# Splitting the 128x128 matmuls of a graph propagation into four of 128x32, so that one stage of TensorE uses a single array shape

## The chip, the core and the metric

The kernel runs on one core of one Trainium2 chip. The metric is the device time of one execution in microseconds (us), as a median over several executions. Three executions of the kernel before took 3994.35, 3999.09 and 4004.58 us; their median is 3999.09 us.

## The reference

The input is a graph with N = 10000 nodes and E = 160000 edges, and a feature vector of D = 128 numbers for each node. The features are propagated seven times along the edges; each result is kept, and a small attention block then works on the eight vectors of each node.

```python
h = x
toks = [x]
for _ in range(7):
    msg = h[src] * deg_inv_sqrt[src, None] * deg_inv_sqrt[dst, None]
    h = _segment_sum(msg, dst, N)
    toks.append(h)
tok = jnp.stack(toks, axis=1)                      # (N, 8, D)
t = _layernorm(tok, axis=-1)
# q, key, v = t @ wq, t @ wk, t @ wv;  attn = softmax(q key^T / sqrt(D))
o = tok + (attn @ v) @ wo
alpha = softmax(layernorm(o) @ w_r)                # over the 8 tokens
out = sum over k of alpha[:, k] * o[:, k]
```

## The kernel before, in words

The program has four parts: a sort of the edges (up to about 420 us), hop 1 with the building of the matrices (to about 1200 us), hops 2 to 7 (to about 3297 us) and the attention (the rest). The change touches hops 2 to 7 alone.

A hop is written as matrix products with zeros and ones. The table `tab` of the node vectors lies in SBUF: 79 blocks of 128 nodes, each vector as a sum of two float16 halves, so 256 columns. The destinations are also taken in 79 tiles of 128 nodes, one pass of `block` (L492) for each. For one tile, 18 groups (`NG`) of up to 128 edges are handled in 9 pairs:

- **Gather** (L541): for each group four matmuls, each with a 128x32 piece of the matrix `w` as the stationary operand and one source block `tab[:, s, :]` (128x256) as the moving operand. They go to the four 32-row quarters of a PSUM tile `p`, so to the four 32-column strips of the array. There are 72 of them in a tile. The pool of `p` has six buffers (L636), and a tile takes nine, one for each pair.
- **Eviction** (L544): `p` is copied to SBUF as float16, `eb`, by ScalarE for the pairs 0, 2, 4, 5 and 7 and by VectorE for 1, 3, 6 and 8 (the rule is in the call at L701).
- **Scatter** (L517 in `scat`): for each group one matmul with a 128x128 piece of `w` and `eb` (128x256), summed up in the PSUM tile `acc`. There are 18 in a tile.
- **Fetched and overflow rows** (`fetched`, L503): two more 128x128 matmuls into `acc`, with rows `og` that GpSimd has fetched from the table in HBM by an indirect DMA (L488), one with a piece of `w` and one with the matrix `Sov`. In the first two tiles of a hop (`late`) the overflow matmul stands in `close` (L530) instead, since its rows are written only at the end of the hop before.
- **Closing** (L532 and `fin`, L675): VectorE adds the two halves to `s`, ScalarE scales it into the new table (L677), VectorE makes the second half (L678) and a maximum (L680), and ScalarE issues the DMA of the new rows to HBM (L158). For the blocks from 72 on it issues a second one, to `tabh` (L162); these seven tiles come first in a hop (`order`, L685). GpSimd scales `s` for the output (L573).

The order on TensorE follows from `block`: all 72 gathers of a tile, then the fetched and overflow matmuls, then what is left over of the tile before (its last four scatter matmuls, `lag` is 2 pairs), then 14 scatter matmuls of the tile itself. Each engine works through its own list in the order of the program, and waits on semaphores. The matrix `w` of a tile (592 KB) is loaded by a DMA on SyncE's queue (L700) into one of five buffers. `fetch` for the tile two ahead is held back by a small copy (L487) that waits for the eviction of pair 4.

Of the kernel before, what the change touches and what calls it, by code (L numbers as in the profile page):

```python
# [20 lines left out]
NG = 18  # L21
NI = 1
# [15 lines left out]
class Hops:  # L38
# [453 lines left out]
    def block(self, t, w, tab, og, pend, lag, runs, first, evac, fin, lead=False, late=False, mid=None, ahead=None):  # L492

        nc, V, A, T, G = self.nc, self.nc.vector, self.nc.scalar, self.nc.tensor, self.nc.gpsimd
        m = 257 if first else 256
        acc = []


        def fetched(i, start=False, stop=False):
            W = w[:, (NG + i) * 128:(NG + i + 1) * 128] if i < NI else self.Sov[:, t, :]
            T.matmul(acc[0][:, :256], W, og[i], start=start, stop=stop)  # L503
            if first:
                T.matmul(acc[0][:, 256:257], W, self.ones16, start=False, stop=False)

        def begin():
            acc.append(self.pacc.tile([128, 512], F32, name="acc", tag="acc"))
            for i in range(NI if late else NI + 1):
                fetched(i, start=i == 0)  # L510

        def scat(e, jj):
            if not acc:
                acc.append(self.pacc.tile([128, 512], F32, name="acc", tag="acc"))
            for j in range(e.shape[1]):
                J = 2 * jj + j
                T.matmul(acc[0][:, :m], w[:, J * 128:(J + 1) * 128], e[:, j, :m], start=first and J == 0,  # L517
                         stop=J == NG - 1 and not (first or late))
                if first and J == 0 and not lead:
                    for i in range(NI):  # L520
                        fetched(i)

        def close():
            if first:
                if lead:
                    for i in range(NI):
                        fetched(i)
                T.matmul(acc[0][:, 256:257], self.Sov[:, t, :], self.ones16, start=False, stop=False)
            if first or late:
                T.matmul(acc[0][:, :256], self.Sov[:, t, :], og[NI], start=False, stop=True)  # L530
            s = self.fp.tile([128, 128], F32, name="s")
            V.tensor_reduce(s, acc[0][:, 0:256].rearrange("p (h d) -> p d h", h=2), axis=X, op=ALU.add)  # L532
            fin(t, s, acc[0])

        def gather(jj):
            n = min(2, NG - 2 * jj)
            p = self.pg.tile([128, 2, 2, 128], F32, name="p")
            for j in range(n):
                for q in range(4):
                    s = 4 * (2 * jj + j) + q  # L540
                    T.matmul(p[32 * q:32 * q + 32, j], w[:, NJ * 128 + s * CAP:NJ * 128 + (s + 1) * CAP], tab[:, s, :], start=True, stop=True)  # L541
            e = self.ebuf[self.eb_i % len(self.ebuf)]
            self.eb_i += 1
            (A.copy if evac(jj) else V.tensor_copy)(e[:, :n, 0:256], p[:, :n].rearrange("p j h d -> p j (h d)"))  # L544
            pend.append(lambda: scat(e[:, :n], jj))

        jj = 0
        for i, n in enumerate(runs):
            for _ in range(n):
                gather(jj)  # L550
                if jj == 4 and not first and not mid:
                    ahead(self.ebuf[(self.eb_i - 1) % len(self.ebuf)][:, 0, 0:1])
                jj += 1
            if mid:
                mid(0)
            if not first:
                begin()
                if mid:
                    ahead()
            while len(pend) > lag:  # L560
                pend.pop(0)()
            if mid:
                mid(1)
            if i == len(runs) - 1:
                pend.append(close)
            yield
# [642 lines left out]
```

## Time and profile before

| | before |
|---|---|
| median of three executions | 3999.09 us |
| span of the profiled execution, first to last instruction | 3993.2 us |
| TensorE busy (matmuls) | 3698.2 us, 69691 matmuls |
| TensorE weight loads | 3031.4 us, 69691 |
| VectorE busy | 3307.4 us |
| ScalarE busy | 2652.0 us |
| GpSimd busy | 1775.7 us |

The device time of the profiled execution itself is not shown, only its span, which lies 1.2 us under the shortest of the three times. In the profile PE is TensorE's matmuls, PEld its weight loads, DVE is VectorE, ACT ScalarE, POOL GpSimd, SP SyncE; "ACTq" and the like are DMA issues by that engine. The profile models the end of a matmul, and matmuls overlap: one of 256 columns has 0.27 us in the trace though the next may start 0.11 us after it. So the pace of TensorE is to be read from starts, and its busy share says little.

### The profile page before, as it was taken

What the parts mean: (1) busy time and instruction counts of PE and PEld (TensorE: products, weight loads), DVE (VectorE), ACT (ScalarE), POOL (GpSimd) and SP (SyncE); (2) the same over time, 40 slices, a digit from 0 to 9 for tenths busy, and PEclk for the clock granted to TensorE, in tenths of its full rate; (3) what the DMA queues carried; (4) which work ended last, traced back from release to release, by engine and by line L of the source; (5) the groups of instructions that cost most, each with busy time, mean ns of one, the idle gap of its engine ahead of it and who ended that gap; (6) DMA issues with size and microseconds to landing.
All of it is one profiled execution on the core that took longest, in us unless ns stands there. A gap on an engine that the chain in (4) does not pass through costs nothing. (4 is left out here: it accounts for less than half of the span.)

```text
span 3993.2 us, 164299 instructions
## 1 busy us (share of the span) xinstructions
PE 3698.2 (93%) x69691; PEld 3031.4 (76%) x69691; DVE 3307.4 (83%) x6948; ACT 2652.0 (66%) x6799; POOL 1775.7 (44%) x2355
## 2 busy tenths in 40 slices
PE   4776799999979999999999999999999997999997
PEld 3765666667648888888888888888888886888875
DVE  8998999999967777777777777777766665999998
ACT  6774366666666666666666666666655557888884
POOL 0000333333326665666666666666656661222222
PEclk8988999999989999999999999999999998999998
DMA  3100444444456666666666666666656653222220
GB/s 107 30 1 1 129 152 153 146 153 149 145 179 198 201 200 196 202 202 203 192 203 203 195 201 201 202 199 203 203 182 187 188 168 91 76 78 78 75 74 13
DMA packets 320622, 594.87 MB, mean 149 GB/s; under 512 B 55623, under 2 KB 213541, under 8 KB 314629
## 3 DMA queue, kind: packets, MB, share of 16 engines
q1 hardware_dynamic: 219749, 477.37, 38.5%
q0 software_dynamic: 35392, 72.55, 6.0%
q10 hardware_dynamic: 64736, 34.38, 3.0%
q8 instruction: 546, 8.95, 0.9%
q14 instruction: 199, 1.63, 0.1%
HBM read 455.43 MB, written 128.67 MB: 146 GB/s over the span
## 5 line engine op out<-in xcount | busy, mean ns | idle before, releaser
L544 ACT CAST eb<-p 128x512 f16<-128x512 f32 x3081 | 1591.0, 602 | 694.6 <-PE p L541 670.7
L544 DVE CAST eb<-p 128x512 f16<-128x512 f32 x1896 | 1179.3, 683 | 346.7 <-PE p L541 331.1
L541 PE MATMUL p<-tab,w 128*32 128x256 f16 x39816 | 1284.9, 274 | 39.8 <-ACT eb L544 22.1
L517 PE MATMUL acc<-eb,w 128*128 128x256 f16 (+1 forms) x9954 | 1239.8, 273 | 12.7 <-DVE indeg L595 10.3
L541 PEld LDWEIGHTS <-w 128*32 128x32 fp8e4 x39816 | 1001.3, 96 | 240.1 <-issue 181.6
L517 PEld LDWEIGHTS <-w 128*128 128x128 fp8e4 x9954 | 953.1, 98 | 174.5 <-issue 61.6
L488 POOL DMA_INDIRECT og<-tabh,oidx x553 | 638.4, 1154 | 732.4 <-DVE vi L440 400.6
L488 POOL DMA_INDIRECT og<-tabd,oidx x541 | 563.3, 1041 | 433.8 <-PE acc L530 268.3
L573 POOL TENSOR_SCALAR r<-s,ctok 128x128 f32<-128x128 f32 x474 | 296.1, 625 | 33.6 <-DVE s L532 18.5
L678 DVE SCALAR_TENSOR_TENSOR tab<-s,c,tab 128x128 f16<-128x128 f32 x395 | 139.2, 352 | 183.1 <-ACT tab L677 182.1
L677 ACT ACTIVATE tab<-s,c 128x128 f16<-128x128 f32 x395 | 158.5, 401 | 182.7 <-DVE s L532 182.4
L487 POOL COPY og<-eb 128x1 f16<-128x1 f16 x457 | 85.1, 186 | 426.7 <-ACT eb L544 426.6
L315 ACT ACTIVATE o<-oh,d2s 128x79 f16<-128x79 f16 x800 | 204.7, 373 | 80.9 <-PE ta L329 80.9
L532 DVE TENSOR_REDUCE s<-acc 128x128 f32<-128x256 f32 x553 | 228.5, 413 | 27.4 <-PE acc L530 20.4
L918 ACT ACTIVATE junk<-x 128x128 f32<-128x128 f32 x625 | 245.0, 394 | 0.0
L476 DVE TENSOR_TENSOR w<-dsl,iof 128x2432 fp8e4<-128x2432 f16 x79 | 211.7, 2679 | 0.0
L976 POOL TENSOR_TENSOR p<-e,in 128x512 f32<-128x512 f32 (+1 forms) x40 | 40.8, 1021 | 342.8 <-DVE e L974 342.8
L904 PEld LDWEIGHTS po<-v,pT 128*128 128x128 f32 x1250 | 159.0, 193 | 44.7 <-issue 27.6
L329 PE MATMUL ta<-o,ro 128*128 128x158 f16 x1250 | 119.7, 267 | 77.9 <-DVE ro L325 77.8
L893 PE MATMUL pv<-Wv,xT 128*128 128x131 f32 x1250 | 175.7, 284 | 4.5 <-ACT xT L873 3.8
L329 PEld LDWEIGHTS <-ro 128*128 128x128 f16 x1250 | 114.5, 113 | 82.2 <-DVE ro L325 82.0
L904 PE MATMUL po<-v,pT 128*128 128x128 f32 x1250 | 166.8, 277 | 7.7 <-DVE o L910 7.7
(277 smaller groups left out, 4642.3 us busy)
## 6 DMA issues: line engine op xcount, KB each, us to landing
w<-gsd SPq DMA_DIRECT2D x474, 592.0 KB
gsd<-w SPq DMA_DIRECT2D x79, 592.0 KB
rb<-srow SPq DMA_DIRECT2D x79, 576.0 KB
tok<-r SPq DMA_DIRECT2D x546, 64.0 KB
x<-tok SPq DMA_DIRECT2D x266, 128.0 KB
tabd<-tab ACTq DMA_DIRECT2D x395, 64.0 KB
og<-tabh,oidx POOLq DMA_INDIRECT x553
og<-tabd,oidx POOLq DMA_INDIRECT x541
```

The source lines that it names most:

```text
L315: A.activation(o[:, j - a, NK:, i], oh[:, j, :, i], AF.Copy, scale=d2s[:, c0:c0 + 1])
L329: T.matmul(ta, ro[:, j - a, :, i], o[:, j - a, :, i], start=j + i == 0, stop=j + i == NP)
L476: V.tensor_tensor(w[:, :NJ * 128].rearrange("p (j d) -> p j d", d=128), dsl[:, g, :, None].to_broadcast([128, NJ, 128]), self.iof1[:, None ...
L488: self.nc.gpsimd.indirect_dma_start(out=o, out_offset=None, in_=src[0] if i == NI else src[1], in_offset=bass.IndirectOffsetOnAxis(ap=self ...
L517: T.matmul(acc[0][:, :m], w[:, J * 128:(J + 1) * 128], e[:, j, :m], start=first and J == 0, stop=J == NG - 1 and not (first or late))
L532: V.tensor_reduce(s, acc[0][:, 0:256].rearrange("p (h d) -> p d h", h=2), axis=X, op=ALU.add)
L541: T.matmul(p[32 * q:32 * q + 32, j], w[:, NJ * 128 + s * CAP:NJ * 128 + (s + 1) * CAP], tab[:, s, :], start=True, stop=True)
L544: (A.copy if evac(jj) else V.tensor_copy)(e[:, :n, 0:256], p[:, :n].rearrange("p j h d -> p j (h d)"))
L573: self.nc.gpsimd.tensor_scalar(r, s, ct[:, t:t + 1], None, op0=ALU.mult)
L893: T.matmul(p[:, g - a, :], S[i]["xT"][:, g, :], Wv, start=True, stop=True)
L904: T.matmul(p[:, g - a, :], PT[i % 2][:, g, :], S[i]["v"][:, g, :128], start=True, stop=True)
L918: A.activation(j, S[i]["x"][:, g, :], AF.Square, bias=S[i]["x"][:, g, 0:1], scale=-1.0, accum_out=S[i]["sq"][:, g:g + 1])
```

## The change

A helper `onto` takes the place of the plain call in the three places that write `acc`. In hop 1 (`first`) it makes the same single matmul as before. In hops 2 to 7 it makes four: column strip c of the stationary matrix, 32 columns wide, goes to the strip c of the array and to the rows c to c + 31 of `acc`. All four have the same moving operand, and the flags `start` and `stop` of the one that they replace. In these hops the 20 matmuls of 128x128 in a tile become 80 of 128x32, as the gathers already are; the numbers that are added stay the same.

```diff
+        def onto(W, rhs, start, stop):
+
+            if first:
+                T.matmul(acc[0][:, :rhs.shape[-1]], W, rhs, start=start, stop=stop)
+                return
+            for c in range(0, 128, 32):
+                T.matmul(acc[0][c:c + 32, :rhs.shape[-1]], W[:, c:c + 32], rhs, start=start, stop=stop, tile_position=(0, c))
+
         def fetched(i, start=False, stop=False):
             W = w[:, (NG + i) * 128:(NG + i + 1) * 128] if i < NI else self.Sov[:, t, :]
-            T.matmul(acc[0][:, :256], W, og[i], start=start, stop=stop)
+            onto(W, og[i], start, stop)
...
                 J = 2 * jj + j
-                T.matmul(acc[0][:, :m], w[:, J * 128:(J + 1) * 128], e[:, j, :m], start=first and J == 0,
-                         stop=J == NG - 1 and not (first or late))
+                onto(w[:, J * 128:(J + 1) * 128], e[:, j, :m], first and J == 0, J == NG - 1 and not (first or late))
...
             if first or late:
-                T.matmul(acc[0][:, :256], self.Sov[:, t, :], og[NI], start=False, stop=True)
+                onto(self.Sov[:, t, :], og[NI], False, True)
```

## The prediction

> **What bounds the kernel now.** I read the page first, for the share of each engine over time.
>
> ```profile
> span 3993.2 us, 164299 instructions
> PE 3698.2 (93%) x69691; PEld 3031.4 (76%) x69691; DVE 3307.4 (83%) x6948; ACT 2652.0 (66%) x6799; POOL 1775.7 (44%) x2355
> PE   4776799999979999999999999999999997999997
> L517 PE MATMUL acc<-eb,w 128*128 128x256 f16 (+1 forms) x9954 | 1239.8, 273 | 12.7 <-DVE indeg L595 10.3
> q8 instruction: 546, 8.95, 0.9%
> w<-gsd SPq DMA_DIRECT2D x474, 592.0 KB
> ```
>
> Each slice is 100 us, and a queue has packets, MB and its share. PE shows 9 through hops 2 to 7, which are 474 tiles (one load of `w` each). A busy PE isn't yet a bound, so I next asked for the engines in stretches inside each of the six hops.
>
> ```profile
> core 0: us, PE busy (x) PEld busy (x) DVE busy (x) ACT busy (x) POOL busy (x), PEclk, DMA share, GB/s
> 1240.00:1540.00 300.00, 300.00 (x6307) 254.44 (x6300) 230.96 (x482) 202.39 (x413) 190.80 (x275) 1.00 0.65 202
> 1650.00:1890.00 240.00, 240.00 (x5060) 203.74 (x5059) 184.57 (x385) 161.94 (x330) 152.96 (x220) 1.00 0.65 202
> 1965.00:2240.00 275.00, 275.00 (x5796) 233.37 (x5795) 211.50 (x441) 185.51 (x378) 175.07 (x252) 1.00 0.65 202
> 2295.00:2400.00 105.00, 105.00 (x2224) 89.19 (x2220) 80.65 (x168) 70.74 (x145) 66.85 (x98) 1.00 0.65 203
> 2410.00:2590.00 180.00, 180.00 (x3800) 152.61 (x3789) 138.65 (x289) 121.59 (x249) 113.97 (x164) 1.00 0.65 203
> 2645.00:2940.00 295.00, 295.00 (x6210) 250.32 (x6203) 227.34 (x474) 199.11 (x407) 187.29 (x269) 1.00 0.65 202
> 3005.00:3290.00 285.00, 284.88 (x5996) 241.46 (x5989) 183.71 (x327) 165.93 (x328) 179.58 (x259) 1.00 0.59 182
> ```
>
> PE is covered throughout, at clock 1.00; DVE has 77%, ACT 67%, POOL 64%, the DMA engines 65%. The stretches hold 35393 matmuls; at 92 for a tile that is 385 tiles in 1680 us, 4.37 us each. Third, the timeline of one such tile shows what the 4.37 us consist of.
>
> ```profile
> 2408.41 2.15 PE L541 MATMUL p<-tab,w 128*32 128x256 f16 x72
> 2408.92 2.54 ACT L544 CAST eb<-p 128x512 f16<-128x512 f32 x5 [1.00 <-PE p L541]
> 2409.08 2.48 DVE L544 CAST eb<-p 128x512 f16<-128x512 f32 x4 [0.58 <-PE p L541]
> 2410.49 0.28 PE L503 MATMUL acc<-og,w 128*128 128x256 f16 x1
> 2410.61 0.27 PE L503 MATMUL acc<-og,Sov 128*128 128x256 f16 x1
> 2410.72 2.13 PE L517 MATMUL acc<-eb,w 128*128 128x256 f16 x18
> ...
> 2411.49 0.41 DVE L532 TENSOR_REDUCE s<-acc 128x128 f32<-128x256 f32 x1
> 2411.93 0.40 ACT L677 ACTIVATE tab<-s,c 128x128 f16<-128x128 f32 x1 [0.47 <-DVE s L532]
> 2412.37 0.35 DVE L678 SCALAR_TENSOR_TENSOR tab<-s,c,tab 128x128 f16<-128x128 f32 x1 [0.47 <-ACT tab L677]
> 2412.63 0.28 DVE L680 TENSOR_REDUCE mx<-tab 128x1 f32<-128x128 f16 x1
> 2412.75 0.33 ACTq L158 DMA_DIRECT2D tabd<-tab  x1
> ...
> 2412.78 0.84 PE L541 MATMUL p<-tab,w 128*32 128x256 f16 x24
> ```
>
> A row's length runs from the first start to the last modelled end. The 18 scatter matmuls take 2.13 us, the last of them 0.273, so 17 steps take 1.857: 0.1092 us each. The 72 gathers go in 18 sets of four that start nearly together (four strips of the array at once): (2.15 - 0.273)/17 = 0.110 for a set. Gathers and scatters thus cost the same, one slot of 0.109, and a tile has 18 + 20 = 38 slots: 38 x 0.1092 = 4.15 us. The period is 4.37. The missing 0.22 us sits at the two seams. The last scatter starts at 2410.72 + 1.86 = 2412.58 and the next gather at 2412.78: 0.20, not 0.11. The last gather set starts at 2408.41 + 2.15 - 0.27 = 2410.29, the first matmul of 128x128 at 2410.49: 0.20 again. The rest, about 0.02, is a slower first slot behind each seam (2410.49 to 2410.61 is 0.12). The list of waits says whether every tile pays this.
>
> ```profile
> PEld L503 <- issue: 98.9, 468, 0.2
> PEld L541 <- issue: 93.6, 440, 0.9
> PEld L541 <- DMA tok<-r: 10.5, 50, 0.2
> PE acc L530 <- DMA ogl<-tabd,oidx: 9.1, 5, 3.9
> ```
>
> Before L503 the weight loader is idle 468 times, 0.21 us each; before L541 490 times, 0.21 each. It is the same at both seams, though different things could be waited for there, and nearly always put down to no releaser. I take it that TensorE empties itself when the shape of the tiles in the array changes.
>
> **The change, part by part.** *Seams.* With one shape in hops 2 to 7 both go. A tile shrinks from 4.37 to 38 x 0.1092 = 4.15 us, by 0.22. For the 385 tiles of the stretches that is 84.7 us.
>
> *Tiles outside the stretches*, 474 - 385 = 89, are mostly the starts of the hops. One of those:
>
> ```profile
> 2262.25 2.29 PE L541 MATMUL p<-tab,w 128*32 128x256 f16 x72
> 2262.47 0.45 ACTq L162 DMA_DIRECT2D tabh<-tab  x1
> 2263.02 2.54 ACT L544 CAST eb<-p 128x512 f16<-128x512 f32 x5 [1.33 <-PE p L541]
> ...
> 2266.76 0.62 PE L541 MATMUL p<-tab,w 128*32 128x256 f16 x16
> ```
>
> Here ACT issues a second DMA, its first eviction starts 0.77 us after the first gather (0.51 in the tile above), and the gathers take 2.29 instead of 2.15: they wait for one of the six `p`. The period is 4.51. ACT's loop sets it together with PE: its restart counts from the gather start before, so what PE saves in one period comes back as a later `p` in the next, and on average half is kept, 0.11 of 0.22. Tiles that wait for a fetch (L530, five times) keep nothing. Between 0 and 0.22 for each of the 89, I take 0.14, most of them being between these ends: 12 us. Together 84.7 + 12 = 97 us.
>
> *The split matmuls themselves* are new: 128x32, float8 weights, four with the same moving operand, adding to `acc`. Nearest rows:
>
> ```profile
> 3409.53 0.83 PE L893 MATMUL pv<-Wv,xT 128*128 128x131 f32 x6
> 3410.30 0.64 PE L930 MATMUL sm<-rb,same 128*32 128x256 f32 x8
> 3410.75 0.40 PE L930 MATMUL sm<-lb,same 128*32 128x128 f32 x8
> ...
> 3411.95 1.08 PE L1072 MATMUL pf<-o,Ab 128*32 128x128 f32 x32
> 3360.93 1.30 PE L924 MATMUL ps<-xT,uT 128*32 128x32 f32 x128
> 3360.93 1.19 PEld L924 LDWEIGHTS ps<-xT,uT 128*32 128x32 f32 x128
> ```
>
> L930 has four strips with one moving operand. Its second set of four starts at about 3410.30 + 0.64 - 0.38 - 0.02 (the stagger inside a set) = 3410.54, the set after it at 3410.75: 0.21 for 256 columns. One matmul of 128x128 with 131 such columns takes (0.83 - 0.27)/5 = 0.112 (L893), so 0.22 for 256: four strips go in the time of one. L1072 adds up in half of its 32 and does 8 sets in 1.08 - 0.27 = 0.81, about 0.1 each. So a split slot costs 0.109 by the gathers; that is the lower end too, as nothing here shortens the streaming of 256 columns. For the upper end: L930's first set takes 0.24 instead of 0.21, a seventh more. Were every split slot that long, a tile would lose 20 x 0.109/7 = 0.31 us, 0.09 over the gain: 3999 + 474 x 0.09 = 4042. But that is the set behind a seam, slow as the gathers' own first slot (0.12) is; I take 0.109.
>
> *Issue.* A tile goes from 92 x 2 = 184 instructions on TensorE to 152 x 2 = 304, one per 13.7 ns if 4.15 us are to be kept. The gathers keep that pace now (8 in 0.109 us), for 1.9 us at a time. L924 issues 128 matmuls and 128 weight loads in 1.10 us, 4.3 ns each. Longer stretches at this pace don't occur, so its lower price is 0. The instruction queue brought 8.95 MB in 546 packets for 139382 instructions, 64 bytes each and 255 in a packet; the change needs 474 x 120 / 255 = 223 packets more, 3.7 MB on top of 595. The price is 0 while a packet comes every 4.15 x 255/304 = 3.5 us (one in 6.1 us now); at 3.67 us the gain is gone.
>
> By the Trainium skill, "Runtime: NRT & Kernel Launch", section "Instruction fetch mechanics", fetching is hidden because the sequencer needs some 20 cycles for an instruction; its page "TensorE: Matmul & The Clock Gate" gives that sequencer 1.2 GHz, so by my estimate 304 x 16.7 ns = 5.07 us for a tile, 0.70 over today's period, and a sum of about 4330 us. The 4.3 ns of L924 speak against it, as far as 256 instructions reach.
>
> *DVE.* Its chain in the tile runs from 2409.08 to 2412.91, with ACT's L677 in it, and its next eviction can start 0.67 us after the next gather, then 2413.23: 0.32 left of 0.54. *ACT* is tighter. Its DMA issue ends at 2413.08, and an eviction starts 0.10 after such an issue (2262.92 to 2263.02): 2413.18, which is 4.77 after the gather start, or 0.62 into the next tile. At 0.77 the gathers lost 0.14, so from about 0.63 they lose. It just fits, with 0.01 to spare; I cost it at 0. If this cover goes, half of each further delay is lost per tile, so 0.1 us costs 474 x 0.05 = 24 us. *POOL* has 187 us of work in 295 us, 2.8 us in a tile, and each fetch is asked for two tiles ahead. *DMA* at 0.65 goes to 0.65 x 4.37/4.15 = 0.68, and 202 to 213 GB/s. Both cost nothing; if the loads of `w` became the limit, the period would stay at what they allow, between 4.15 and 4.37.
>
> **Sum.** The profiled execution has a span of 3993 us, which lies 6 under the median of the runs. 3993 - 97 = 3896 for the span, 3902 to 3903 for the median: I say 3903. The ends: all 474 tiles gain 0.22, which is 104 us and 3895; ACT's loop lasts 0.2 longer than read, 48 us are lost, and it is 3950.
>
> **The rivals.** *ACT's loop becomes the bound*: its own period was read as hardly under 4.15, from rows rounded to 0.01, and evictions may get slower when PE writes without a pause. For it: the hop starts, where one more issue of 0.45 us stops PE. Against: ACT still has 33% idle. A loop 0.05 to 0.2 us longer gives 3915 to 3950. *The seams stay*: the 0.20 comes from starting another accumulation or from a semaphore at the first matmul, not from the shape; then 3999. Against: the same 0.20 at both seams, where other data and other buffers are waited for. *Issue decides* (the other side): PE's sequencer or its fetches don't keep 73 instructions per us for 2000 us. From 4.37/304 = 14.4 ns each it is slower than before; a packet only every 4.1 us would make a tile 4.1 x 304/255 = 4.89 us and the time 3999 + 474 x 0.52 = 4245 us. For it: the best the trace has over a long time is 184 in 4.37 us. Against: L924, and that no gather waits for instructions. The skill's 20 cycles would be this rival too.
>
> **How the numbers follow.** Forecast (seams go, PE sets 4.15): 0.72, 3895 to 3912. ACT's loop: 0.15, 3912 to 3950. Seams stay: 0.04. Issue decides or split slots are longer: 0.09, from 4000 up. Range: 3890, a few us under the lower end for the spread of medians (runs differ by 10 us), up to 3940, most of the ACT case. A measurement can tell 0.3% (12 us) from no change. Faster 0.87, same 0.04, slower 0.09.
>
> **What would show it.** Right: between L503 and L541 starts of 0.11, no idle time of 0.21 before either on the weight loader, a period of 4.15 us, 304 instructions of TensorE per tile. ACT's loop: gathers longer than 2.14 us in the middle of a hop, and "PE p from ACT eb" in the waits. Issue: sets of four more than 0.109 apart everywhere, with no releaser. The prediction is wrong if the split slots or the feeding of PE cost over 0.01 us per slot.

## The result, and the profile after

The changed kernel takes 4247.09 us in the median, the kernel before, measured with it, 4001.01: a ratio of 1.0617, 95% interval 1.0598 to 1.0636. It is slower by 6%, where 2.4% faster was forecast. The profiled execution took 4254.48 us, with a span of 4252.7.

The page of the changed kernel (L548 is now the gather, L507 the split matmuls, L504 the unsplit ones of hop 1, L551 the eviction):

```profile
span 4252.7 us, 221179 instructions
PE 3694.2 (87%) x98131; PEld 3237.0 (76%) x98131; DVE 3333.7 (78%) x6948; ACT 2658.2 (63%) x6799; POOL 1771.3 (42%) x2355
PE   5776899999978888888888888888888897999997
q8 instruction: 768, 12.58, 1.2%
```

PE was at 9 through hops 2 to 7 and is at 8 now; all other engines have lost share too. So TensorE has become idle, and nobody else has become the bound. Two of the stretches by engine and the list of waits over the hops say the same:

```profile
1650.00:1890.00 240.00, 209.73 (x7320) 198.54 (x7313) 165.59 (x337) 142.16 (x289) 134.34 (x194) 1.00 0.58 178
2645.00:2940.00 295.00, 257.37 (x8963) 243.06 (x8958) 203.81 (x425) 174.21 (x354) 163.38 (x233) 1.00 0.58 178
```

```profile
PEld L507 <- issue: 294.7, 292, 3.4
PE acc L507 <- issue: 222.7, 264, 2.0
PEld L548 <- issue: 90.5, 214, 1.6
PE p L548 <- issue: 38.3, 90, 1.4
```

At 152 matmuls a tile, 7320 in 240 us are 4.98 us each; 4.37 was the period before and 4.15 the forecast. (These stretches were laid into the quiet parts of the hops of the kernel before; here they hold some starts of hops as well.) What TensorE waits for is "issue", nothing that the profile shows. Evictions and fetched rows stand in the whole list of waits with 11 us in all before its gathers and sums, and loads of `w` not at all. Now the timeline of the weight loads, each of which stands for two instructions, since each has its matmul:

```profile
2417.10 0.33 PEld L548 LDWEIGHTS <-w 128*32 128x32 fp8e4 x14 [1.34 <-issue]
2417.59 0.60 PEld L548 LDWEIGHTS <-w 128*32 128x32 fp8e4 x23 [0.15 <-issue]
2418.18 0.12 PEld L507 LDWEIGHTS <-w 128*32 128x32 fp8e4 x4
2418.29 0.12 PEld L507 LDWEIGHTS <-Sov 128*32 128x32 fp8e4 x4
2418.40 1.98 PEld L507 LDWEIGHTS <-w 128*32 128x32 fp8e4 x72
2420.36 0.34 PEld L548 LDWEIGHTS <-w 128*32 128x32 fp8e4 x11
2421.39 1.64 PEld L548 LDWEIGHTS <-w 128*32 128x32 fp8e4 x61 [0.70 <-issue]
2422.94 0.20 PEld L507 LDWEIGHTS <-w 128*32 128x32 fp8e4 x4
2423.05 0.20 PEld L507 LDWEIGHTS <-Sov 128*32 128x32 fp8e4 x4
2423.16 1.71 PEld L507 LDWEIGHTS <-w 128*32 128x32 fp8e4 x59
2425.14 0.33 PEld L507 LDWEIGHTS <-w 128*32 128x32 fp8e4 x13 [0.27 <-issue]
```

Count from stop to stop: 14 + 23 + 4 + 4 + 72 + 11 = 128 loads, then 61 + 4 + 4 + 59 = 128. With the matmuls that is 256 instructions each time, wherever in the tile that falls: one stop in the middle of the gathers, the next one in the middle of the scatters. A packet of the instruction queue holds 12.58 MB / 768 = 16.4 KB, at 64 bytes 256 instructions. (The gap of 0.15 at 2417.59 stands before the 50th gather, about where the seventh `p` is needed, and is taken for a wait for it.) Between stops TensorE keeps the pace that was forecast: 72 loads in 1.98 us, 0.027 us for a load and its matmul. And where the seams were, starts follow at the pace of the slots: the next gather after the scatters of this tile is in the row at 2420.36, right behind.

In the stretch from 1650 to 1890 us the list of DMA queues has 57 packets of instructions, so one every 4.21 us, and 40 in the kernel before, one every 6.0. First the changed kernel, then the one before:

```profile
q8 instruction: 57, 0.93, 1.6%
```

```profile
q8 instruction: 40, 0.66, 1.3%
```

In the records of the single packets, TensorE starts again 1.39 us (median) after the end of a packet, in hops 2 to 7 nearly always between 1.2 and 1.8, and packets start 4.18 us apart in the mean, 3.25 at the least and 5.2 or more in the slowest twentieth. TensorE uses 256 instructions in 3.5 us. So my theory after the result was the feed: the program comes in packets of 256 instructions, the next only some four us after the last, and whoever uses one faster waits.

### The profile page after: what moved, and what is told of

Read it like the earlier page. It is cut to its first block, busy times and chain, and to the rows that moved or that the text cites. A ratio compares the mean times of both kernels' runs of the same rounds, so it can differ in the third digit from the quotient of the medians.

```text
span 4252.7 us, 221179 instructions
## 1 busy us (share of the span) xinstructions
PE 3694.2 (87%) x98131; PEld 3237.0 (76%) x98131; DVE 3333.7 (78%) x6948; ACT 2658.2 (63%) x6799; POOL 1771.3 (42%) x2355
## 3 DMA queue, kind: packets, MB, share of 16 engines
q8 instruction: 768, 12.58, 1.2%
## 4 chain that ended last, share of the span: by engine, by line
PE 67%; DVE 19%; issue 8%; DMA 3%; ACT 2%; SPq 0%; ACTq 0%; POOL 0%; DVEq 0%; POOLq 0%
PE acc L507 25%; PE p L548 23%; PE pv L900 3%; PE po L911 3%; DVE w L476 3%; PE pu L889 3%; DVE ux L208 2%; PE ta L329 2%; DVE w L473 2%; DVE R L201 2%; PE pt L879 2%; DVE oh L195 1%; DVE ro L325 1%; PE acc L504 1%; DVE o L201 1%
## 5 line engine op out<-in xcount | busy, mean ns | idle before, releaser
L551 ACT CAST eb<-p 128x512 f16<-128x512 f32 x3081 | 1598.2, 600 | 841.1 <-PE p L548 783.3
L551 DVE CAST eb<-p 128x512 f16<-128x512 f32 x1896 | 1193.5, 685 | 484.1 <-PE p L548 463.0
L548 PE MATMUL p<-tab,w 128*32 128x256 f16 x39816 | 1357.3, 274 | 84.7 <-issue 38.9
L507 PE MATMUL acc<-eb,w 128*32 128x256 f16 x34128 | 1108.9, 273 | 190.8 <-issue 189.3
L548 PEld LDWEIGHTS <-w 128*32 128x32 fp8e4 x39816 | 1096.8, 97 | 211.8 <-issue 179.0
L507 PEld LDWEIGHTS <-w 128*32 128x32 fp8e4 x36024 | 1058.7, 97 | 261.2 <-issue 259.9
L504 PE MATMUL acc<-eb,w 128*128 128x257 f16 x1422 | 226.4, 276 | 10.7 <-DVE indeg L602 9.2
L507 PE MATMUL acc<-og,Sov 128*32 128x256 f16 x1848 | 175.1, 273 | 25.9 <-issue 23.9
L507 PE MATMUL acc<-og,w 128*32 128x256 f16 x1896 | 177.3, 273 | 13.4 <-issue 10.3
```

Source lines behind the costliest of these rows:

```text
L504: T.matmul(acc[0][:, :rhs.shape[-1]], W, rhs, start=start, stop=stop)
L507: T.matmul(acc[0][c:c + 32, :rhs.shape[-1]], W[:, c:c + 32], rhs, start=start, stop=stop, tile_position=(0, c))
```

## The experiments

**Fewer instructions at the same shape.** The first two runs keep the single shape and all 38 slots, and issue only two or three of the four strips.

```diff
+        def onto(W, rhs, start, stop, strips=128):
-            for c in range(0, 128, 32):
+            for c in range(0, strips, 32):
...
-                onto(w[...], e[...], first and J == 0, ...)
+                onto(w[...], e[...], first and J == 0, ..., 64 if J < NG - 1 else 128)    # 96 in the second
```

> The changed kernel, but in hops 2 to 7 seventeen of the 18 scatter groups of a tile issue only two of their four strips (rows 64 to 127 of their sums are left out); the 38 slots and the single shape stay. Instructions of TensorE per tile fall from 304 to 236. Feed theory (instructions come in packets of 256, one at a time, every 4.18 us in the mean; TensorE stops where it uses them faster): 4.15 us of work now use a packet in 4.15 x 256/236 = 4.50 us, slower than they come, so the stops nearly go and the seams' gain shows: 3900 to 3935 us. Rival, the loss belongs to the split sums into acc themselves: half of the strips, half of the loss of 344 us (4247 - 3903): about 4070 us. Seams not worth 0.22 us a tile: about 4000.

> As with two strips, but three of four strips in seventeen of the 18 groups (rows 96 to 127 are left out): 270 instructions per tile. Feed theory: a tile can't be shorter than 270/256 x 4.18 = 4.41 us, against 4.37 in the kernel before: about 4018 us, 4000 to 4060. Rival, the split sums cost: three quarters of the loss: about 4160 us.

Two strips: 3905.28 us, ratio 0.978 (0.9765 to 0.9798), within what the feed theory gave and 165 us from the rival. Three: 4035.99, ratio 1.0105 (1.0085 to 1.0125); the feed theory said 4018, the rival 4160. Two strips in the timeline, and the list of waits over the hops:

```profile
2404.55 0.31 PE L507 MATMUL acc<-og,w 128*32 128x256 f16 x4
2404.66 0.30 PE L507 MATMUL acc<-og,Sov 128*32 128x256 f16 x4
2404.79 1.93 PE L507 MATMUL acc<-eb,w 128*32 128x256 f16 x34
...
2408.72 0.29 PE L507 MATMUL acc<-og,w 128*32 128x256 f16 x4
```

```profile
PEld L548 <- issue: 19.4, 64, 1.0
PEld L507 <- issue: 10.4, 6, 5.5
```

A tile takes 4.17 us, as forecast (4.15), and the idle time before the weight loads falls from 385 to 30 us. So the seams were worth what the prediction said, and neither ScalarE's loop nor the split sums (here half of them) stand in the way of that gain; the 88 us fall short of the 97 forecast by 9, less than the 30 us of stops that are left.

**More instructions without the change.** This run takes the kernel before, with unsplit scatters, and doubles the gathers.

```diff
-                    T.matmul(p[32 * q:32 * q + 32, j], w[...], tab[:, s, :], start=True, stop=True)
+                for h in range(2):                       # in hops 2 to 7
+                    for q in range(4):
+                        T.matmul(p[32 * q:32 * q + 32, j, h], w[...], tab[:, s, 128 * h:128 * h + 128], start=True, stop=True)
```

> The kernel before, scatter untouched and both seams kept; in hops 2 to 7 each gather matmul of 256 columns is done as two of 128, with the weights loaded again for each. The array streams as many columns; instructions per tile rise from 184 to 328. Feed theory: 328/256 x 4.18 = 5.36 us a tile instead of 4.37: about 4470 us, with stops 256 instructions apart. Rival, the loss belongs to the split sums into acc: nothing of it is here, so about 4000 us, up to 4100 if the array needs some ns more for each matmul.

Measured: 4422.66 us, ratio 1.107 (1.1051 to 1.1095); the feed theory said 4470, the rival 4000. The weight loads in its timeline, with the evictions of the same tile:

```profile
2406.62 2.76 ACT L551 CAST eb<-p 128x512 f16<-128x512 f32 x5 [0.99 <-PE p L548]
2406.78 1.68 PEld L548 LDWEIGHTS <-w 128*32 128x32 fp8e4 x117 [0.28 <-issue]
2407.10 2.48 DVE L551 CAST eb<-p 128x512 f16<-128x512 f32 x4 [0.90 <-PE p L548]
2408.56 0.10 PEld L503 LDWEIGHTS <-w 128*128 128x128 fp8e4 x1
2408.57 0.10 PEld L503 LDWEIGHTS <-Sov 128*128 128x128 fp8e4 x1
2408.68 0.97 PEld L517 LDWEIGHTS <-w 128*128 128x128 fp8e4 x9
2410.52 0.97 PEld L517 LDWEIGHTS <-w 128*128 128x128 fp8e4 x9 [0.87 <-issue]
```

117 + 1 + 1 + 9 = 128 again, and the stop falls between two scatters of the old, whole shape. It ends at 2410.52, and the tile's last eviction had ended at 2407.10 + 2.48 = 2409.58, so these scatters don't wait for `eb`. Nothing of the change is in this kernel: more instructions alone make such stops and a loss of this size. A small part of it may be the granted clock, which was 0.97 to 0.99 in this run's stretches where the kernel before had 1.00; 3% of a tile's 4.37 us are 0.13, and a tile lost about 0.9 (429 us over 474 tiles).

**Why a packet takes four us.** Two runs take DMA traffic away from the changed kernel, with its 304 instructions per tile.

```diff
-                    w = self.gsp.tile(...); nc.sync.dma_start(w, self.GSd[t])
+                    if len(kept) < 5:
+                        w = self.gsp.tile(...); nc.sync.dma_start(w, self.GSd[t]); kept.append(w)
+                    w = kept[n % 5]
...                                             # second run, besides: hops 3 to 7 reuse og, no new rows to HBM
+                    if k > 2:
+                        for m in range(n + 2, min(n + 3, NT)): og[m][:] = self.kog
+                        return
```

> The changed kernel, but the matrices w are loaded only five times in all and used again by all tiles (so nearly all sums of hops 2 to 7 are of the wrong matrix); 304 instructions per tile as in the changed kernel. This takes away most of the DMA traffic in hops 2 to 7. Feed theory with a packet that is slow because of that traffic: it comes in 3.3 us as at the quickest places of the trace, under the 3.5 that TensorE needs, the stops go: 3900 to 3920 us. Feed theory with a latency that the traffic has little part in: 4200 to 4250 us, with packets still near 4.1 us apart. Split sums cost: 4247.

> As with five loads of w (304 instructions per tile), and in hops 3 to 7 also no fetched rows (those of hop 2 are used again) and no new table rows written to HBM, so that hardly any DMA traffic is left but the output rows. Feed theory with a part due to traffic: five loads brought packets from 4.18 to 3.80 us apart in the mean; without the rest they should come 3.3 to 3.5 apart, under the 3.5 that TensorE needs: 3900 to 3940 us. If what is left above 3.5 is not traffic: as with five loads, 4027.

Five loads: 4027.13 us, ratio 1.0083 (1.0061 to 1.0105). Without the rest too: 4014.06, ratio 1.0038 (1.0022 to 1.0054). Each lies between its cases, the second near the upper one. The instruction queue from 1650 to 1890 us, first for five loads, then without the rest:

```profile
q8 instruction: 63, 1.03, 1.8%
```

```profile
q8 instruction: 65, 1.06, 2.0%
```

A packet every 3.81 and every 3.69 us, after 4.21 in the changed kernel. The DMA engines were at 0.58 of their time there, at 0.25 and 0.07 here. So the traffic of `w` has a part, some 0.4 us of a packet's 4.2, and the expectation that all of what is over 3.5 us comes from traffic was wrong: with next to none the feed still takes 3.7.

The records of the single packets show where the time goes. Counting 256 instructions from stop to stop gives the moment at which TensorE takes up each packet. Means from 1650 to 1890 us:

| us | changed | five loads | without the rest |
|---|---|---|---|
| from taking up one packet to the start of the next one's transfer | 1.77 | 1.34 | 1.19 |
| the transfer | 1.06 | 1.08 | 1.15 |
| from its end until TensorE takes it up | 1.38 | 1.38 | 1.38 |
| sum | 4.21 | 3.80 | 3.72 |

The traffic of `w` lengthens neither the transfer nor what follows it, but the time before it. In these three runs no transfer of the stretch starts sooner than 1.05 us after TensorE took up the packet before. In the kernel before, where the feed is not short, it starts between 1.4 us before that moment and 1.7 us after it. So the feed works about one packet ahead, and the three parts follow each other. What the sequencer does in the first and the third part no run here tells.

**Whether other strips help.** Two strips of 64 columns would need only 224 instructions in a tile.

```diff
-            for c in range(0, 128, 32):
-                T.matmul(acc[0][c:c + 32, ...], W[:, c:c + 32], rhs, ...)
+            for c in range(0, 128, 64):
+                T.matmul(acc[0][c:c + 64, ...], self.id64[:, c:c + 64], rhs, ...)
```

> The changed kernel, but the 20 matmuls of a tile are split into two of 128x64 instead of four of 128x32, with a constant float16 matrix as the stationary operand (so the sums of hops 2 to 7 are not those of the graph; the shapes and counts are what is looked at). 224 instructions per tile: far from the limit of the feed. If any change of the strip width empties the array, both seams are back: 4.37 us a tile, about 3994 to 4000. If only the whole 128-wide shape does, they are gone: 4.15 us, about 3900.

Measured: 4004.45 us, ratio 1.0018 (1.0007 to 1.0028). Its timeline:

```profile
2402.27 2.15 PE L548 MATMUL p<-tab,w 128*32 128x256 f16 x72
2404.35 0.41 PE L507 MATMUL acc<-og,id 128*64 128x256 f16 x4
2404.59 2.13 PE L507 MATMUL acc<-eb,id 128*64 128x256 f16 x36
2406.65 2.15 PE L548 MATMUL p<-tab,w 128*32 128x256 f16 x72
```

4.38 us a tile; the gathers' last set starts at 2404.15 and the first strip of 64 at 2404.35, 0.20 later. Going between strips of 32 and of 64 costs the same seam as going to the whole shape. The stationary operand changes here from float8 to float16 too, at the same place, so this run alone does not tell the width from the type; in the kernel before the type was float8 on both sides of a seam.

**Fewer seams.** The other way is to keep the instructions few and the seams few. The first try splits by tile.

```diff
-            if first:
+            if first or t % 2:
```

> The changed kernel, but only the tiles of even number are split, the others use 128x128 as before: nothing is left out. Two tiles have 488 instructions and two seams instead of four: 8.52 us of work. If the feed only has to keep up in the mean (488/256 x 4.18 = 7.97 us): 4.26 a tile, about 3945 us. If a packet is asked for only when the one before it begins to be used, so that no stretch of 256 may be shorter than 4.18 us: 448 of the 488 instructions follow each other at 13.7 ns, 192/488 of the packets lie wholly in there and cost 0.68 each, 0.75 of them in two tiles: 0.5 us lost for 0.22 gained, about 4.51 a tile, about 4065 us.

Measured: 4051.18 us, ratio 1.0133 (1.0113 to 1.0153), close to the second case, but for another reason, since the expectation had miscounted. Each scatter stage begins with matmuls left over from the tile before, which are of the other kind here:

```profile
2401.72 2.14 PE L548 MATMUL p<-tab,w 128*32 128x256 f16 x72
2403.78 0.28 PE L504 MATMUL acc<-og,w 128*128 128x256 f16 x1
2403.90 0.27 PE L504 MATMUL acc<-og,Sov 128*128 128x256 f16 x1
2404.11 0.62 PE L507 MATMUL acc<-eb,w 128*32 128x256 f16 x16
2404.66 1.70 PE L504 MATMUL acc<-eb,w 128*128 128x256 f16 x14
2406.29 2.15 PE L548 MATMUL p<-tab,w 128*32 128x256 f16 x72
...
2410.67 2.22 PE L548 MATMUL p<-tab,w 128*32 128x256 f16 x72
```

Four seams in this tile and two in the next, six in place of four. 76 slots and six seams are 8.30 + 0.66 = 8.96 us; from 2401.72 to the gather two tiles on, 2410.67, are 8.95. It says nothing on the feed, and gives the price of a seam once more. Two seams lie inside each scatter stage here, where only the shape and the sum change; in the kernel before the sum changes at the first of these places (2410.61 to 2410.72 in its timeline) without a seam. So the next two kernels split by stage.

```diff
         def begin():
+            self.whole = t % 2 == 1                  # in the second: t % 3 != 1
...
-            if first:
+            if first or self.whole:
```

> The changed kernel, but only every other scatter stage is split, and with all that stands in it, the four matmuls left over of the tile before too (splitting by tile put two shapes into each stage: six seams in two tiles, which alone give 8.30 + 6 x 0.11 = 8.96 us, and 8.95 was measured). Nothing is left out. Two tiles have 488 instructions and two seams: 8.52 us of work. Feed has to keep up only in the mean (488/256 x 4.18 = 7.97 us): 4.26 a tile, about 3942 us, and a kernel faster than both. Feed must bring each 256 within the time that they take: 448 of the 488 follow each other at 13.7 ns, 0.75 packets in two tiles lie wholly in there and cost up to 0.68 us each: up to 0.5 us lost for 0.22 gained, up to 4.51 a tile, 4000 to 4065 us.

> As with every other stage, but one stage in three is split: three tiles have 672 instructions and four seams, 12.89 us of work. Feed in the mean: 672/256 x 4.18 = 10.97 us, no loss, 4.30 a tile, about 3960 us. Each packet for itself: again 448 instructions in a row once in three tiles, up to 0.5 us lost for 0.22 gained, up to 4.47 a tile, 3990 to 4042 us.

Every other stage: 3974.95 us, ratio 0.9944 (0.9928 to 0.9961). One in three: 3973.30, ratio 0.9936 (0.9916 to 0.9955). Both leave nothing out, and both are 0.6% faster than the kernel before. Two tiles of the first:

```profile
2402.73 2.15 PE L549 MATMUL p<-tab,w 128*32 128x256 f16 x72
...
2404.93 2.14 PE L507 MATMUL acc<-eb,w 128*32 128x256 f16 x72
2406.89 2.14 PE L549 MATMUL p<-tab,w 128*32 128x256 f16 x72
...
2411.25 2.15 PE L549 MATMUL p<-tab,w 128*32 128x256 f16 x72
```

From 2402.73 to 2411.25 are 8.52 us, as worked out, and no stop. Both times lie between the cases. 237 split stages save 0.22 us each, 52 us, of which 23 arrive, so about 0.12 is lost for each; 158 save 35, of which 25 arrive, 0.06 lost for each. A run of 448 instructions isn't punished by 0.5 us, then, but the mean isn't all that counts either: something bears a short run in part. In the stretch from 1650 to 1890 us the packets of the first of these kernels land 1.2 to 3.7 us before TensorE takes them up, 2.4 in the mean, against 1.4 throughout in the changed kernel. So the feed gets up to some 2.4 us ahead, it seems while the unsplit stages run, and a split stage uses that up. How the 0.12 and the 0.06 follow from it was not worked out.

The last run halves the seams without splitting anything: the gathers of two tiles, then the scatters of both.

```diff
+                    ba = blk(n, pend, 0, True); next(ba)        # gathers of tile n
+                    bb = blk(n + 1, pb, 2, True); next(bb)      # gathers of tile n + 1
+                    for _ in ba: pass                           # scatters of n
...
+                    for _ in bb: pass                           # scatters of n + 1
```

> The kernel before with unsplit matmuls and nothing left out, but in hops 2 to 7 the gathers of two tiles stand one after the other and then their scatters, so that two tiles share two seams; 20 eb buffers instead of 14 and one more og. No instruction is added. Seams worth 0.11 us each: 474 x 0.11 = 52 us less, about 3942, if the evictions keep up with 18 pairs in a row; each 0.1 us per pair of tiles that TensorE waits for p takes back 24 us. Seam theory false: no gain, about 3994 or slower.

Measured: 4009.02 us, ratio 1.0031 (1.0021 to 1.0041).

```profile
2402.13 4.43 PE L541 MATMUL p<-tab,w 128*32 128x256 f16 x144
...
2406.72 0.60 PE L517 MATMUL acc<-eb,w 128*128 128x256 f16 x4
2407.49 2.14 PE L517 MATMUL acc<-eb,w 128*128 128x256 f16 x18 [0.17 <-issue]
...
2411.31 4.43 PE L541 MATMUL p<-tab,w 128*32 128x256 f16 x144
```

144 gathers should last 35 x 0.1092 + 0.28 = 4.10 us and last 4.43. In the single records the steps that are too long stand 16 matmuls apart, from the 72nd on (the last one 8), and mostly end 0.05 us after the end of an eviction: the six buffers of `p` run out. That costs 0.33 us, and a pair saves 0.22. By its time alone this run would also fit the expectation's other case, no gain from fewer seams; what speaks against that case is the price of a seam in the runs above. The stop before 2407.49 ends 1.34 us after a packet of instructions: 288 gather instructions in a row have brought the feed in as well.

## Why the prediction was wrong

- *What bounds the kernel*: right. 38 slots of 0.109 and two seams made the period, and the run with two strips shows 4.17 us when nothing else is short.
- *Seams, 97 us*: right in mechanism and nearly in size. 88 us were gained by two strips with a few stops left; six seams cost six times 0.11. That the price hangs on the change of shape is shown; that TensorE empties itself there stays an inference. The rival that the seams stay fell in the changed kernel's own timeline.
- *The split matmuls themselves, 0.109 for a slot*: right; four strips with one moving operand, adding up, go at the gathers' pace between the stops.
- *Issue, price 0*: this is the step that failed. The prediction worked out that a packet of instructions would have to come every 3.5 us and that at 3.67 the gain is gone, and then took the lower end. One came every 4.2 us. Two rows were read as covering this which couldn't: the gathers keep the pace for 144 instructions and L924 for 256, both no more than one packet holds. The prediction's own rival with "a packet only every 4.1 us" gave 4245 us, and the kernel landed at 4247, but the rival had a share of a chance of 0.09, on the strength of those two rows. That it came within 2 us is partly luck: its 4.1 was taken from no row. The packet records of before would have warned: the closest two packets are 3.3 us apart (in the attention; in hops 2 to 7 they are 4.1), but no three come within 9.3 us, so 3.5 us a packet, one after the other, had nowhere been seen.
- *The Trainium skill's rule in that rival*, "Runtime: NRT & Kernel Launch", section "Instruction fetch mechanics": blocks of 16 KiB, 256 instructions, are what the stops show, 16.4 KB and 256. That the fetching is hidden, since the sequencer needs some 20 cycles for an instruction, is not what they show: TensorE used one in 13 ns between the stops, and the fetch was what it waited for. By the 20 cycles the time would have been 4330; measured were 4247.
- *ACT's loop*: did not bind. It was read as just fitting into 4.15 us, and with two strips a tile takes 4.17 with only 2.0 us of waits for evictions before the gathers of all hops; so the loop is hardly longer than 4.17, and how much shorter it is no run here shows.
- *DMA and POOL cost nothing*: right where the gain came through (two strips). DMA had a part all the same, which the prediction had not looked for: beside the loads of `w` the instruction packets come 0.4 us further apart, not because a transfer takes longer but because the next one starts later.

## What to carry to other kernels

Before trading a shape for more, smaller matmuls, divide 256 by the number of TensorE instructions per us that the new loop needs over many us, weight loads counted, and compare with the closest that the trace shows three or more instruction packets in a row (9.4 us for three here, before the change). That is a pace known to work, not yet the limit. Two that came close prove nothing (3.3 us was seen before, 4.2 was what the feed kept up), nor does a burst that fits into one packet. Here the limit was about 4.2 us for 256 beside 180 GB/s of other traffic, 61 instructions per us. Where a seam of shapes costs 0.11 us, removing some of the seams (every second or third stage) was worth 0.6%, and removing all of them cost 6%.

## What was not expected of the hardware

- TensorE can wait for its own program: 256 instructions every 4.2 us in the mean under load, 3.7 with hardly any other DMA traffic, against 13.7 ns each (3.5 us) that four strips of 256 columns use.
- In the list of waits such stops stand as "issue" on PE and PEld, 292 times before L507, as the seams did before (468 times 0.21 us). The difference is in the distances: seams at one place of the loop, all of one length; fetches 128 weight loads apart, or a multiple of that, at any place and mostly from 0.25 to 2 us long.
- The feed works about one packet of 256 instructions ahead: its next transfer starts 1.4 us before TensorE takes up the packet before it at the earliest, when nothing is short, and 1.8 us after that in the mean in the changed kernel.
- Strips of 64 columns next to strips of 32 cost the same seam, 0.20 us from start to start, as the whole array next to strips of 32 (with the type of the stationary operand changing too).
